# Layer B's step rebuilt: output product in four column quarters, new memory turned by VectorE, tails in batches of sixteen, softmax in stages

## The chip, the core and the metric

The kernel runs on one core of one Trainium2 chip. Five engines work side by side, each through its own instruction stream: TensorE (PE: matmuls, and PEld: the loads of the stationary operand), VectorE (DVE), ScalarE (ACT), GpSimd (POOL) and SyncE (SP), which issues the transfers here. SBUF is the working memory of 128 partitions, and TensorE writes to PSUM. The metric is the time on the device in microseconds (us); lower is better.

## What is computed

Two layers in turn, A B A B, each behind a LayerNorm and added to the residual `x` of 2048 tokens by 640. A is a linear-memory attention over four segments; the change hardly touches it. B is a recurrence over 64 segments of 32 tokens. Each segment sees 8 memory rows and its 32 tokens, 40 rows in all; 32 heads of 128:

```python
for s in range(n_seg):
    xs = x[:, s * seg_len:(s + 1) * seg_len, :].copy()
    h = jnp.concatenate([mem, xs], axis=1)
    q = jnp.einsum('btd,dhe->bhte', h, Wq)
    k = jnp.einsum('btd,dhe->bhte', h, Wk)
    v = jnp.einsum('btd,dhe->bhte', h, Wv)
    scores = jnp.einsum('bhqe,bhke->bhqk', q, k) * scale
    scores = jnp.where(mask[None, None], scores, -1000000000.0)
    p = _softmax(scores, axis=-1)
    o = jnp.einsum('bhqk,bhke->bhqe', p, v)
    o = jnp.einsum('bhte,hed->btd', o, Wo)
    mem = o[:, :M, :].copy()
    outs.append(o[:, M:, :])
```

The first 8 rows of a segment's output are the memory of the next one, so that the 64 steps of a layer can't be done side by side. What doesn't hang on the memory can: normalised tokens, and the projections of tokens whose place in the step is free.

## The kernel before

**Layer B, one step.** `layer_B` (L778) runs 64 steps. Step `s` finishes segment `s` while it projects 32 rows: the 8 memory rows of segment `s` beside the first 24 tokens of segment `s + 1`. The last 8 tokens of a segment, its *tail*, are projected ahead, in batches over several segments, and kept in DRAM. TensorE's order in a step is the order of the program text (`_OrdNC` chains each of TensorE, ScalarE, VectorE and GpSimd in that order):

1. `thin_mm`: keys and queries (`b_Ka`, `b_Qa`, `b_Kb`, `b_Qb`), each 20 matmuls of 512 columns, with 32 rows of the stationary operand in each of four column groups of the array; the column groups run side by side.
2. `transp4` and `scatter`: four blocks turned on TensorE (`b_TPak` and so on), copied by DVE (memory rows) and ACT (next segment's rows) into `QT` and `KT`.
3. `mask_mm` and `scores`: 128 small matmuls into two PSUM tiles `b_SP`, one for 16 heads each.
4. Softmax on DVE and ACT: for each tile maximum, subtraction and exponential, tile after tile; then sums, reciprocal, product (the second tile's on GpSimd, L1186 on), and `p_turn`, which turns the weights on DVE into `b_PTa` and `b_PTb`.
5. Meanwhile on TensorE values (`b_Va`, `b_Vb`) and one unit of tail projections (`tail_unit`, `b_tail`: 8 heads x 5 chunks, 64 columns = 8 segments x 8 tokens).
6. `pv`: weights by values (`b_OTP`, 64 matmuls), copied to `OTsb` by DVE and ACT.
7. `od_chunk(0)` (a part of the output product of four earlier segments' tails, `b_OPSd`), then the step's output product `o_mm` into `b_OPS` (L974): 64 matmuls of 320 columns. The 640 output columns are two halves of interleaved 64-column pieces. Four column groups of the array take two heads x two halves, so rows 0 to 63 and 64 to 127 of `b_OPS` hold partial sums that have still to be added. Then `od_chunk(1)`.
8. New memory: ACT copies `b_OPS` to `b_msb` in three parts, and small matmuls with a 0/1 matrix `selm` (`b_MT`) turn the memory rows and add the two partial sums (the *fold*), DVE writes them into the next step's columns (`b_HX`). In between stand pieces of `vtail_unit` (value projections of tails, 20 matmuls of 256 columns).
9. `x_out`: two adds on DVE (one for each half of the partial sums) with the residual rows `XO`, and two stores.

A tail unit's result is stored by `tail_evac` to `QKd` (DRAM, one row of 128 x 512 for each segment) and fetched a step ahead by `tails_load` into one buffer, from which GpSimd copies it into `QZ` and `KT` (`tails_copy`) behind its part of the softmax.

**LayerNorm for B** comes in groups of 128 tokens: `ln_load`, `ln_norm` (DVE, with one power on GpSimd between), and a step later `ln_spread` (five turns on TensorE, two copies on ACT into `HX`, the tokens, and `TX`, the tails).

**Entry of a layer B.** All 8 tail units of the first batch, then keys and queries of the first segment, `load_B_wo`, value tails, and the first steps; weights `wv` and `wo` are read again for each layer B, as their space serves layer A in between.

**Transfers** are issued on SP, one queue in order.

Of the kernel before, what the change touches and what calls it, by code (L numbers as in the profile page):

```python
# [37 lines left out]
def alloc_consts(tc, ctx):  # L38
# [10 lines left out]
    C.selm = cp.tile([128, 2, 8], BF16, name="b_sel")  # L49
# [122 lines left out]
def build_masks(G, C, pool):  # L172

    G.tensor_tensor(out=C.selm[:, 0, :], in0=C.identb[:, 24:32], in1=C.identb[:, 88:96], op=ALU.add)
    G.tensor_tensor(out=C.selm[:, 1, :], in0=C.identb[:, 56:64], in1=C.identb[:, 120:128], op=ALU.add)
# [70 lines left out]
def layer_A(nc, tc, C, W, x_src, x_dst, src_is_bf16, nseg=4, out_bf16=False, xb_dst=None, load_w=None, side_loads=None):  # L246
# [7 lines left out]
    with ExitStack() as ctx:  # L254
# [105 lines left out]
        def out_stage_b(n_, tt, halves=(0, 1)):  # L360
# [20 lines left out]
            xnb = w1l.tile([128, D], BF16, name="a_xnb")  # L381
            if n_ == nseg - 1:
                nc.scalar.copy(xnb[:], xnew[:])
            else:
                K("xnb").gpsimd.tensor_copy(xnb[:], xnew[:])
# [367 lines left out]

def load_B_resident(nc, W, B_Wq, B_Wk, k, after):

    c, r = divmod(k, 8)
    t, src = ((W.wk, B_Wk), (W.wq, B_Wq))[r % 2]
    h = r // 2
    nc.gpsimd.tensor_copy(t[0:1, c, 1024 * h:1024 * h + 1], after[0:1, 0:1])
    nc.sync.dma_start(t[:, c, 1024 * h:1024 * h + 1024], src[128 * c:128 * c + 128, 8 * h:8 * h + 8].rearrange("p h e -> p (h e)"))  # L760


def load_B_wv(nc, W, B_Wv):
    for c in range(NCH):
        nc.sync.dma_start(W.wv[:, c, :], B_Wv[128 * c:128 * c + 128].rearrange("p h e -> p (h e)"))
# [12 lines left out]
def layer_B(nc, tc, C, W, x_src, xb_src, x_dst, mem0, B_Wv, B_Wo, nsteps=64, out_bf16=False, tag=""):  # L778
# [4 lines left out]
    NT = nsteps // 8  # L783
    QKd = tc.dram_tile([nsteps, 128, 512], BF16, name=f"b_QKd{tag}")
    VTd = tc.dram_tile([nsteps, 8, 4096], BF16, name=f"b_VTd{tag}")
    with ExitStack() as ctx:
# [4 lines left out]
        hp = pool("b_hx", 4)  # L791
# [21 lines left out]
        mask5, selm = C.mask5, C.selm  # L813
        QZ = st.tile([128, 32, 32], BF16, name="b_QZ")
        HXz = st.tile([128, NCH, 1, 32], BF16, name="b_HXz")
        OTdef = [wk.tile([128, 32, 32], BF16, name=f"b_OTdef{i}") for i in range(2)]

        def init_state():
            XO_ = bx.tile([64, 320], F32, name="b_XO", tag="XO")
            nc.vector.memset(XO_[:], 0.0)  # L820
            XOd_ = bx.tile([64, 320], F32, name="b_XOd", tag="XOd")
# [20 lines left out]
        def ln_load(g, home=None):  # L842
            pool_, tg = home or (bx, "xt")
            xt = pool_.tile([128, D], BF16, name="b_xt", tag=tg)
            nc.sync.dma_start(xt[:], xb_src[128 * g:128 * g + 128, :])
            ln_xt[g] = xt

        def ln_norm(g):
            xt = ln_xt[g]
            f = layernorm_tile(nc, sml, C, xt[:], xt[:], "b_ln")  # L850
            if g in (0, 2) and not entered:
                info = mybir.DependencyInfo(mybir.DependencyClass.NoSync, mybir.DependencyReason.SCHED_ONLY)
                tc.add_manual_dep(f.ins, (C.after2 if g else C.after).ins.name, info, reason="order")
            ln_ready.append(g)

        def ln_spread(g):
            xt = ln_xt.pop(g)
# [3 lines left out]
            HX[g] = hp.tile([128, NCH, 4, 32], BF16, name="b_HX", tag="HX")  # L861
            T, half = divmod(g, 2)
            if half == 0:
                TX[T] = tx.tile([128, NCH, 8, 8], BF16, name="b_TX", tag="TX")
            nc.scalar.copy(TX[T][:, :, 4 * half:4 * half + 4, :], tps[:, :, :, 24:32])
            nc.scalar.copy(HX[g][:, :, :, 8:32], tps[:, :, :, 0:24])

        def cols_of(u):
            if u == nsteps:
                return HXz[:, :, 0, :]  # L870
            return HX[u // 4][:, :, u % 4, :]
# [26 lines left out]
        def tails_load(s):  # L898
            tl = bx.tile([128, 2, 32, 8], BF16, name="b_tl", tag="tl")
            nc.sync.dma_start(tl[:].rearrange("p a h t -> p (a h t)"), QKd[s])  # L900
            return tl

        def tails_copy(s, tl):
            nc.gpsimd.tensor_copy(QZ[:, :, 0:8], tl[:, 0, :, :])
            nc.gpsimd.tensor_copy(KT[s][:, :, 0:8], tl[:, 1, :, :])
# [9 lines left out]
        def tail_unit(T, k, i0, i1, shared=False):  # L915
            proj, hg = divmod(k, 4)
            Wt = W.wk if proj else W.wq
            if i0 == 0:
                if shared:
                    tail_ps[0] = ps_tile([128, 8, 64], F32, "b_tail")  # L920
                else:
                    tail_ps[0] = po.tile([128, 8, 64], F32, name="b_tail", tag="tail")
            ps = tail_ps[0]
            for i in range(i0, i1):
                h = 8 * hg + i
# [4 lines left out]
        def tail_evac(T, k, eng, home=None, dma=nc.sync.dma_start):  # L930
            proj, hg = divmod(k, 4)
            pool_, tg = home or (wk, "tu")
            tu = pool_.tile([128, 8, 8, 8], BF16, name="b_tu", tag=tg)
            evac(eng, tu[:].rearrange("p s h t -> p h s t"), tail_ps[0][:].rearrange("p h (s t) -> p h s t", t=8),
                 None if proj else SCB)
            o = 256 * proj + 64 * hg
            dma(QKd[8 * T:8 * T + 8, :, o:o + 64].rearrange("s p f -> p s f"), tu[:].rearrange("p s h t -> p s (h t)"))

        def vtail_unit(T, k, c0=0, c1=NCH, ps=None):
# [3 lines left out]
            for c in range(c0, c1):  # L943
                for q in range(4):
                    n = 2 * b4 + q // 2
                    nc.tensor.matmul(ps[32 * q:32 * q + 32, :], lhsT=TX[T][:, c, 4 * (q % 2):4 * (q % 2) + 4, :].rearrange("p s t -> p (s t)"),
# [21 lines left out]
        def wo_half(h, jj2):  # L968
            return W.wo[:, h, :].rearrange("p (c j x) -> p j c x", j=2, x=64)[:, jj2]

        def d_half(rows, jj2):
            return rows.rearrange("t (c j x) -> t j c x", j=2, x=64)[:, jj2]
# [12 lines left out]
        n0 = min(4, NG)  # L985
        for g in range(n0):
            ln_load(g, homes[g])
        load_B_wv(nc, W, B_Wv)
        for g in range(2):
            ln_norm(g)  # L990
        for g in range(2):
            ln_spread(ln_ready.pop(0))
        nc.gpsimd.memset(HX[0][:, :, 0, 0:8], 0.0)
        with nc.allow_non_contiguous_dma(reason="mem0 transpose load (tiny)"):
            for c in range(NCH):
                nc.sync.dma_start(HX[0][:, c, 1, 0:8], mem0[:, 128 * c:128 * c + 128].rearrange("t p -> p t"))
        for k in range(8):
            tail_unit(0, k, 0, 8, shared=True)
            tail_evac(0, k, "act" if k % 2 == 0 else "dve", (((kqp, "kq"),) * 4 + ((w2, "QT"), (w2, "KT"), (wk, "tu"), (w2, "Vth")))[k])
            if k in (0, 2) and n0 > 2:  # L1000
                ln_norm(2 + k // 2)
            if k in (5, 7) and ln_ready:
# [17 lines left out]
        tails_copy(0, tails_load(0))  # L1020
# [7 lines left out]
        if NT > 1:  # L1028
            tail_unit(1, 0, 0, 8, shared=True)
# [3 lines left out]
        def x_out(ops_, XO_, store, nm):  # L1033
            nc.vector.tensor_tensor(out=XO_[:], in0=ops_[0:64, :], in1=XO_[:], op=ALU.add)
            if out_bf16:
                xo = wk.tile([64, 320], BF16, name=f"b_xnb{nm}", tag=f"xnb{nm}")
            else:
                xo = XO_
# [335 lines left out]
```

## Time and profile before

| what | value |
|---|---|
| runs of the kernel | 2619.58, 2614.66, 2613.08 us; median 2614.66 |
| the profiled execution | 2617.2 us |
| its span, first to last instruction | 2615.5 us |
| mean granted TensorE clock | 0.998 |
| first `b_Ka` of the two layers B | 377.7 and 1682.3 us |
| last `b_Ka` of the two layers B | 1287.4 and 2593.6 us |
| the clean step from 510.58 to 524.73 us | 14.15 us: PE busy 14.00, DVE 7.67, ACT 7.24, POOL 1.69 |

Durations come from the profiled execution. A matmul's duration reaches from its start to its modelled end, and matmuls overlap; what a row of matmuls costs PE is read from the distance of their starts. In a timeline a line joins neighbouring instructions of one form: start, time to the end of the last, engine, line of the helper that issued it (L109 for nearly all of layer B), operation, tile written and tiles read, count, and in brackets the idle time ahead of it and what ended it. "issue" there means that the profile shows nothing for which the engine waited. In a row of the groups, the numbers behind the bar are the total busy time in us and the mean duration of one in ns, and behind the second bar the idle time before them.

### The profile page before, as it was taken

The page shows a single profiled execution, that of the slowest core. Times are in us where ns is not written, and L with a number is a line of the kernel's source. Part 1 is how long each engine was busy: PE and PEld are TensorE (multiplying, and loading weights), DVE is VectorE, ACT ScalarE, POOL GpSimd, SP SyncE. Part 2 cuts the span into 40 slices and gives each one's busy share as a digit, 9 for nine tenths or more (in the row PEclk, how much of TensorE's full clock was granted, in tenths as well). Part 3 has the DMA queues.
Part 4 walks back from the last instruction along what each step waited for, and adds up shares of the span by engine and source line. Part 5 has one row for each costly group of instructions (what it writes and reads, how often), then busy time and mean ns, then how long its engine had stood idle before and what let it go on. Part 6 is the DMA issues. An engine that isn't in the chain of part 4 may idle for free.

```text
span 2615.5 us, 144745 instructions
## 1 busy us (share of the span) xinstructions
PE 2492.2 (95%) x64608; PEld 1652.4 (63%) x64608; DVE 1706.5 (65%) x4690; ACT 1529.1 (58%) x3462; POOL 699.0 (27%) x1507
## 2 busy tenths in 40 slices
PE   7999989999999999999989999899999999999998
PEld 5566566666666666666655665666666666666665
DVE  8999855555555555555679998455655555555555
ACT  6988944545555554544379888455545454545443
POOL 5777621111111111111146776111111111111110
PEclk9999999999999999999999999999999999999999
DMA  4122362222222222221220113622222122222110
GB/s 159 46 79 77 103 210 47 46 43 44 48 46 46 47 44 47 41 44 30 64 81 22 63 52 104 200 42 43 43 43 46 41 44 42 43 41 42 39 27 20
DMA packets 325201, 156.21 MB, mean 60 GB/s; under 512 B 245856, under 2 KB 309472, under 8 KB 322784
## 3 DMA queue, kind: packets, MB, share of 16 engines
q1 hardware_dynamic: 324576, 146.95, 22.4%
q8 instruction: 505, 8.27, 1.4%
q14 instruction: 120, 0.98, 0.1%
HBM read 95.15 MB, written 51.71 MB: 56 GB/s over the span
## 4 chain that ended last, share of the span: by engine, by line
PE 64%; DVE 23%; ACT 7%; issue 3%; DMA 2%; SPq 0%; DVEq 0%; POOL 0%; ACTq 0%; POOLq 0%
PE b_OPS L109 11%; DVE a_nm L138 6%; PE b_Ka L109 5%; PE b_Qb L109 5%; PE b_Kb L109 5%; PE b_Qa L109 5%; PE b_vtail L109 3%; PE b_OPSd L109 3%; PE b_SP L109 3%; DVE b_SP L109 3%; ACT a_PT L138 3%; PE a_S L109 2%; DVE b_negmax L109 2%; PE b_OTP L109 2%; DVE b_PTa L109 2%
## 5 line engine op out<-in xcount | busy, mean ns | idle before, releaser
L109 PEld LDWEIGHTS <-b_HX 128*32 128x32 bf16 x15360 | 440.0, 96 | 323.8 <-issue 4.2
L109 POOL TENSOR_TENSOR b_Pn<-b_E,b_rs 128x200 bf16<-128x200 bf16 x128 | 78.0, 609 | 1388.4 <-DVE b_rs L109 1120.5
L138 DVE TENSOR_REDUCE a_nm<-a_S 128x2 f32<-128x512 f32 (+3 forms) x512 | 395.0, 816 | 32.8 <-PE a_S L109 25.2
L138 ACT ACTIVATE a_PT<-a_T 128x1024 bf16<-128x1024 f32 (+1 forms) x384 | 344.9, 902 | 31.6 <-PE a_T L109 23.7
L109 PE MATMUL b_OPS<-b_wo,b_OTsb 128*32 128x320 bf16 x8192 | 305.0, 299 | 3.6 <-issue 2.8
L109 PEld LDWEIGHTS <-b_OTsb 128*32 128x32 bf16 x8192 | 207.1, 96 | 79.3 <-issue 6.5
L109 DVE CAST b_HX<-b_MT 128x8 bf16<-128x8 f32 x372 | 63.8, 172 | 262.9 <-PE b_MT L109 257.6
L138 POOL TENSOR_SCALAR_AFFINE_SELECT a_PT<-a_PT 128x256 bf16<-128x256 bf16 x380 | 187.9, 503 | 128.2 <-ACT a_PT L138 127.2
L109 ACT CAST b_msb<-b_OPS 128x64 bf16<-128x64 f32 x378 | 69.4, 256 | 225.6 <-PE b_OPS L109 225.6
L109 ACT CAST b_kq<-b_Kb 128x512 bf16<-128x512 f32 x128 | 74.9, 585 | 201.7 <-PE b_Kb L109 201.7
L109 DVE COPY b_KT<-b_TPak 128x128 bf16<-128x128 bf16 x128 | 28.7, 225 | 228.3 <-PE b_TPak L109 228.3
L109 DVE TENSOR_SCALAR b_kq<-b_Qa 128x512 bf16<-128x512 f32 x128 | 88.6, 692 | 123.2 <-PE b_Qa L109 120.3
L109 PE MATMUL b_Ka<-b_wk,b_HX 128*32 128x512 bf16 x2520 | 160.4, 379 | 1.8 <-issue 1.4
L109 PE MATMUL b_Va<-b_wv,b_HX 128*32 128x512 bf16 x2520 | 161.6, 380 | 0.0
L109 PE MATMUL b_Vb<-b_wv,b_HX 128*32 128x512 bf16 x2520 | 161.2, 379 | 0.0
L109 PEld LDWEIGHTS <-b_kq 128*128 128x128 bf16 x2080 | 116.9, 98 | 69.3 <-ACT b_kq L109 55.0
L109 PE MATMUL b_Qa<-b_wq,b_HX 128*32 128x512 bf16 x2520 | 159.8, 379 | 0.0
L109 PE MATMUL b_Kb<-b_wk,b_HX 128*32 128x512 bf16 x2520 | 159.7, 379 | 0.0
L109 PE MATMUL b_Qb<-b_wq,b_HX 128*32 128x512 bf16 x2520 | 159.7, 379 | 0.0
L109 DVE CAST b_OTsb<-b_OTP 128x160 bf16<-128x160 f32 (+1 forms) x384 | 133.9, 377 | 29.2 <-PE b_OTP L109 8.5
L109 ACT ACTIVATE b_E<-b_SP 128x200 bf16<-128x200 f32 x256 | 86.3, 337 | 106.9 <-DVE b_SP L109 105.1
L109 PE MATMUL b_vtail<-b_wv,b_TX 128*32 128x256 bf16 x2880 | 135.8, 271 | 5.2 <-issue 5.0
(206 smaller groups left out, 5478.5 us busy)
## 6 DMA issues: line engine op xcount, KB each, us to landing
b_QKd<-b_tu SPq DMA_DIRECT2D x128, 128.0 KB
b_tl<-b_QKd SPq DMA_DIRECT2D x128, 128.0 KB
b_wv<-in_B_Wv_dram SPq DMA_DIRECT2D x10, 1024.0 KB
b_wo<-in_B_Wo_dram SPq DMA_DIRECT2D x16, 640.0 KB
b_Vth<-b_VTd SPq DMA_DIRECT2D x512, 16.0 KB
b_XO<-xres SPq DMA_DIRECT2D x256, 30.0 KB
b_VTd<-b_vt SPq DMA_DIRECT2D x224, 32.0 KB
xres<-a_xnew SPq DMA_DIRECT2D x19, 320.0 KB
```

Of the source, the lines that this page charges most:

```text
L109: r = f(*a, **k)
L138: r = f(*a, **k)
```

## The change

**Output product.** Each head's product goes to the four column groups of the array as four quarters of 160 columns; all heads add up in place. `b_OPS` and `b_OPSd` are [128, 160], row 32 q + t holding token t's quarter q, with no partial sums: 128 matmuls of 160 columns in a step in place of 64 of 320, and 16 in place of 8 in each `od_chunk` part.

**New memory.** DVE copies the first 64 columns of `b_OPS` to `b_msb`, ACT the other 96, and DVE turns `b_msb` in 32 by 32 blocks straight into the next step's columns; the turn also writes 24 columns of tokens that have been used already. The rows of the model dimension are held in another order for that (chunk c, partition 32 q + x is row 160 q + 32 c + x), so the weights of K, Q and V are loaded in that order and layer A writes its bf16 copy of `x` in that order. `selm` and the fold are gone. `b_vtail` stands in one piece behind the output products.

**Tails.** Batches are of 16 segments: a unit is 4 heads, 20 matmuls of 128 columns. 16 units stand ahead of the first step. `QKd` is laid out by unit, so that a store writes 1 KB pieces and a load, now for two segments and issued every second step, reads 128-byte pieces. LayerNorm groups of tokens (every four steps) and of tails (every 16) are apart.

**Softmax.** Both maxima, then both subtractions, then both exponentials.

**Residual rows.** `XO` is loaded whole by one transfer; results go out by four stores in place of two, after one add.

```diff
+            turned = xnb[:].rearrange("p (c q x) -> p q c x", q=4, x=32)
+            plain = xnew[:].rearrange("p (q c x) -> p q c x", q=4, x=32)
...
-                K("xnb").gpsimd.tensor_copy(xnb[:], xnew[:])
+                K("xnb").gpsimd.tensor_copy(turned, plain)
...
+def b_rows(src, c):
+
+    return src.rearrange("(q c x) h e -> c q x h e", q=4, x=32)[c]
...
-    NT = nsteps // 8
+    NT = nsteps // 16
+    NV = nsteps // 8
...
+        def cols_of(u, back=0):
+            t_, i = (HXz, 0) if u == nsteps else (HX[u // 4], u % 4)
+            return t_[:, :, 24 + 32 * i - back:56 + 32 * i - back]
...
         def tails_load(s):
-            tl = bx.tile([128, 2, 32, 8], BF16, name="b_tl", tag="tl")
-            nc.sync.dma_start(tl[:].rearrange("p a h t -> p (a h t)"), QKd[s])
+            tl = bx.tile([128, 2, 8, 2, 4, 8], BF16, name="b_tl", tag="tl")
+            T, i = divmod(s, 16)
+            nc.sync.dma_start(tl[:].rearrange("p a q s h t -> p (a q) (s h t)"), QKd[T][:, :, i:i + 2, :].rearrange("p k s f -> p k (s f)"))
             return tl
...
-            for i in range(i0, i1):
-                h = 8 * hg + i
+            for i in range(4):
+                h = 4 * hq + i
...
-        def o_mm(ops_, src_ap_fn, hpairs, first, last):
-            for n_, h0 in enumerate(hpairs):
-                for e in range(2):
-                    for jj2 in range(2):
-                        k = 2 * e + jj2
-                        nc.tensor.matmul(ops_[32 * k:32 * k + 32, :].rearrange("p (c x) -> p c x", x=64), lhsT=src_ap_fn(h0 + e), rhs=wo_half(h0 + e, jj2),
-                                         start=(first and n_ == 0), stop=(last and n_ == len(hpairs) - 1),
-                                         tile_position=(0, 32 * k), skip_group_check=True)
+        def o_mm(ops_, src_ap_fn, hs, first, last):
+            for n_, h in enumerate(hs):
+                for q in range(4):
+                    nc.tensor.matmul(ops_[32 * q:32 * q + 32, :], lhsT=src_ap_fn(h), rhs=W.wo[:, h, 160 * q:160 * q + 160],
+                                     start=(first and n_ == 0), stop=(last and n_ == len(hs) - 1),
+                                     tile_position=(0, 32 * q), skip_group_check=True)
...
-        for k in range(8):
-            tail_unit(0, k, 0, 8, shared=True)
...
+        for k in range(16):
+            tail_unit(0, k, shared=True)
...
-            nc.vector.tensor_tensor(out=XO_[:], in0=ops_[0:64, :], in1=XO_[:], op=ALU.add)
...
+            nc.vector.tensor_tensor(out=xo[:], in0=ops_[:], in1=XO_[:], op=ALU.add)
...
-            for b, SP in ((0, SPa), (1, SPb)):
-                soft_max(b, SP)
-                soft_sub(b, SP)
-                soft_exp(b, SP)
+            for f in (soft_max, soft_sub, soft_exp):
+                for b, SP in ((0, SPa), (1, SPb)):
+                    f(b, SP)
...
-            if ln_xt_due(s):
-                ln_norm(ln_g(s))
...
-                for ca, cb in parts:
-                    nc.scalar.copy(msb[:, 64 * ca:64 * cb], ops[:, 64 * ca:64 * cb])
-                for pi, (ca, cb) in enumerate(parts):
-                    mt = ps_tile([128, cb - ca, 8], F32, f"b_MT{pi}")
...
-                    nc.vector.tensor_copy(dst[:, ca:cb, 0:8], mt[:])
-                    vtail_some((1, 1, NCH)[pi])
...
+            if ln_due(s):
+                ln_norm(ln_due(s))
+
             if not last:
+                msb = wk.tile([128, 160], BF16, name="b_msb", tag="msb")
+                dst = cols_of(u + 1, 24)
+                nc.vector.tensor_copy(msb[:, 0:64], ops[:, 0:64])
+                nc.scalar.copy(msb[:, 64:160], ops[:, 64:160])
+                for ca, cb in ((0, 2), (2, NCH)):
+                    nc.vector.transpose(out=dst[:, ca:cb, :], in_=msb[:, 32 * ca:32 * cb].rearrange("p (c k) -> p c k", k=32))
+            vps = vtail_unit(vwork[0], vwork[1]) if vwork else None
+            if vunit:
+                vtail_evac(vunit[0], vunit[1], vps, "act")
```

More of the change, by code (lines that the diff above doesn't have):

```diff
@@ L983, in layer_B @@
         entered = []
         homes = [(bx, "xt"), (bx, "XO"), (bx, "XOd"), (bx, "tl")]
-        n0 = min(4, NG)
-        for g in range(n0):
-            ln_load(g, homes[g])
+        for key, home in zip((("T", 0), ("H", 0), ("T", 1), ("H", 1)), homes):
+            ln_load(key, home)
         load_B_wv(nc, W, B_Wv)
-        for g in range(2):
-            ln_norm(g)
-        for g in range(2):
+        ln_norm(("T", 0), C.after)
+        ln_norm(("H", 0))
+        for _ in range(2):
             ln_spread(ln_ready.pop(0))
-        nc.gpsimd.memset(HX[0][:, :, 0, 0:8], 0.0)
+        nc.gpsimd.memset(cols_of(0)[:, :, 0:8], 0.0)
@@ L994, in layer_B @@
         with nc.allow_non_contiguous_dma(reason="mem0 transpose load (tiny)"):
             for c in range(NCH):
-                nc.sync.dma_start(HX[0][:, c, 1, 0:8], mem0[:, 128 * c:128 * c + 128].rearrange("t p -> p t"))
-        for k in range(8):
-            tail_unit(0, k, 0, 8, shared=True)
[L999 to L1002, printed above, removed]
+                for q in range(4):
+                    o = 160 * q + 32 * c
+                    nc.sync.dma_start(cols_of(1)[32 * q:32 * q + 32, c, 0:8], mem0[:, o:o + 32].rearrange("t x -> x t"))
@@ L1063, in od_chunk @@
                 OTd = OTdef[(od["s0"] // 4) % 2]
-                pairs = [8 * k + 2 * p_ for p_ in range(4)]
+                hs = list(range(8 * k, 8 * k + 8))
                 if part is not None:
-                    pairs = pairs[2 * part:2 * part + 2]
-                o_mm(od["ps"], lambda h: OTd[:, h, :], pairs, k == 0 and part != 1, k == 3 and part != 0)
+                    hs = hs[4 * part:4 * part + 4]
+                o_mm(od["ps"], lambda h: OTd[:, h, :], hs, k == 0 and part != 1, k == 3 and part != 0)
                 if part != 0:
@@ L1075, in od_begin, with ln_due @@
         def od_begin(s0, xo, tag="opsd"):
[L1076 to L1082 removed]
+            od.update(s0=s0, n=0, xo=xo, ps=po.tile([128, 160], F32, name="b_OPSd", tag=tag))
+        def ln_due(s):
+            key = ("H", s // 4 + 2) if s % 4 == 1 else ("T", s // 16 + 2) if s % 16 == 11 else None
+            return key if key and key[1] < (NG if key[0] == "H" else NT) else None
         for s in range(nsteps):
```

169 lines of the change are left out of this document (70 added, 99 removed).

## The prediction

> **What bounds the kernel now.** I read the page first, then one layer-B step in the timeline, then the times between the starts of `b_Ka` (one a step), then the stops in PE's stream.
>
> ```profile
> span 2615.5 us, 144745 instructions
> ...
> PE 2492.2 (95%) x64608; PEld 1652.4 (63%) x64608; DVE 1706.5 (65%) x4690; ACT 1529.1 (58%) x3462; POOL 699.0 (27%) x1507
> ...
> q8 instruction: 505, 8.27, 1.4%
> ...
> PE 64%; DVE 23%; ACT 7%; issue 3%; DMA 2%; SPq 0%; DVEq 0%; POOL 0%; ACTq 0%; POOLq 0%
> PE b_OPS L109 11%; DVE a_nm L138 6%; PE b_Ka L109 5%; PE b_Qb L109 5%; PE b_Kb L109 5%; PE b_Qa L109 5%; PE b_vtail L109 3%; PE b_OPSd L109 3%; PE b_SP L109 3%; DVE b_SP L109 3%; ACT a_PT L138 3%; PE a_S L109 2%; DVE b_negmax L109 2%; PE b_OTP L109 2%; DVE b_PTa L109 2%
> ```
>
> TensorE sets the end, and layer B holds most of it: from the first to the last `b_Ka` 909.7 us in the one layer B and 911.3 in the other, 126 step distances of 14.45 us on average. The commonest distance is 14.15, so 0.3 a step is something else. The 505 instruction packets are 16 KB each (8.27 MB); TensorE has 129,216 loads and matmuls, 256 for each packet. A clean step, from `b_Ka` at 510.58 to the next at 524.73:
>
> ```profile
> 518.42 0.34 ACT L109 ACTIVATE b_E<-b_SP 128x200 bf16<-128x200 f32 x1 [0.38 <-DVE b_SP L109]
> 518.78 0.36 DVE L109 TENSOR_REDUCE b_ssum<-b_E 128x5 f32<-128x200 bf16 x1 [0.20 <-ACT b_E L109]
> ...
> 520.91 0.27 PEld L109 LDWEIGHTS <-b_Vth 32*128 32x128 bf16 x32 [0.18 <-DVE b_PTb L109]
> ...
> 521.50 2.35 PE L109 MATMUL b_OPS<-b_wo,b_OTsb 128*32 128x320 bf16 x64
> ...
> 523.96 0.55 ACT L109 CAST b_msb<-b_OPS 128x64 bf16<-128x64 f32 x3 [1.74 <-PE b_OPS L109]
> ...
> 524.46 0.56 DVE L109 CAST b_HX<-b_MT 128x8 bf16<-128x8 f32 x3 [2.37 <-PE b_MT L109]
> ...
> 524.73 1.25 PE L109 MATMUL b_Ka<-b_wk,b_HX 128*32 128x512 bf16 x20
> ```
>
> PE waits in two places: before the second half of `b_OTP` for `b_PTb`, the end of the softmax chain on DVE, which itself waited at 518.78 for the second exponential; and after the output product, for copy, fold and cast. In other steps PE stops in mid stream with nothing to wait for:
>
> ```profile
> 550.09 2.20 PE L109 MATMUL b_OPS<-b_wo,b_OTsb 128*32 128x320 bf16 x57
> ...
> 553.38 0.12 PEld L109 LDWEIGHTS <-b_OTsb 128*32 128x32 bf16 x7 [1.42 <-issue]
> 553.38 0.45 PE L109 MATMUL b_OPS<-b_wo,b_OTsb 128*32 128x320 bf16 x7 [1.09 <-issue]
> ```
>
> Between this stop (551.99) and the like one at 596.06 the trace has 2558 loads and matmuls, 10 x 256 less 2. Between those at 2084.60 and 2129.12 it has 2558 again. At 551.99 the packet for the next 256 instructions ran from 550.49 to 551.96, and PE went on at 553.37, 1.41 us after it; at the other three the distance is 1.57, 1.44 and 1.42. So PE has its instructions in blocks of 256, the next block's packet starts only when it enters a block, and no block may be run in less than the time of that refill. There are 35 such stops of over 0.3 us in the 126 steps, 23.1 us together, 0.18 a step. The refill, counted from entering a block in `b_OTP` or `b_OPS`: 1.15 us to the packet's start (median), 1.1 for it (median 1.116), 1.4 after it: **3.65 us** (single ones 3.1 to 4.3). In slow stretches (`b_Kb`, `b_Vb`) the packet starts up to 0.8 before PE itself gets there, so about 2.5 there.
>
> **The change, part by part** (a step, against 14.15).
>
> Softmax in stages. DVE does both maxima, both subtractions, then the sums. Two dependent pairs lose their gap (end to start 0.10; independent ones overlap by 0.09): second subtraction from 517.95 to about 517.59, second exponential 518.06 to 518.40 (after the first, which starts near 517.77), second sum 518.42 in place of 518.78. All behind it moves along: **-0.36**, bounds 0 and -0.36. It holds if PE gets there in time: tail start 8.54 into the step, 20 matmuls of 128 columns at 56 ns (the row of `b_TPaq`: 4 in 0.22) are 1.12 in place of 40 x 29.4 ns = 1.18, 0.12 to the first `b_OTP` as today, 0.23 for its half: 10.01. `b_PTb` was ready at 10.42 and comes at 10.06, so the shorter tail itself is worth nothing.
>
> Output product. 64 matmuls of 320 columns become 128 of 160, four column groups at a time: groups of four now start 136 ns apart (320 columns are 133.3 of it), so 32 groups x (66.7 + 2.7) = 2.22 against 2.17: **+0.05**; each `b_OPSd` part stays at 0.28. Weight loads don't hold this up: four pairs of `b_SP` (40 columns) start every 25 ns, 6.25 a pair, and 17.3 are needed. The Trainium skill (TensorE: MATMUL & The Clock Gate, Part 1) says that starts never come closer than about 25 ns. By that rule 128 matmuls need 3.2; the row refutes it for column groups, whose starts lie 2 to 4 ns apart.
>
> Step's end. Today 1.05 from the last output matmul to `b_Ka`: `b_OPSd` 0.27, `b_vtail` and the fold's 20 matmuls 0.78. New: the copy can start 0.28 after PE has issued the product (as `b_msb` does), DVE copies 64 columns, turns 64, and `b_Ka` reads.
>
> ```profile
> L109 DVE STREAM_TRANSPOSE b_PTb<-b_Pn 128x64 bf16<-128x64 bf16 x128 | 26.0, 203 | 0.0
> ...
> L109 DVE CAST b_HX<-b_MT 128x8 bf16<-128x8 f32 x124 | 20.7, 167 | 249.8 <-PE b_MT L109 249.7
> ...
> L109 DVE CAST b_OTsb<-b_OTP 128x160 bf16<-128x160 f32 x256 | 83.0, 325 | 29.2 <-PE b_OTP L109 8.5
> ...
> L109 ACT CAST b_msb<-b_OPS 128x64 bf16<-128x64 f32 x126 | 26.7, 212 | 225.6 <-PE b_OPS L109 225.6
> ```
>
> Between 8 and 160 columns DVE pays 1.04 ns a column, so 64 cost 0.23: 0.28 + 0.23 + 0.10 + 0.20 + 0.06 = 0.87, and PE is covered for 0.28 + 20 x 27.3 ns = 0.83. ACT's 96 columns (0.25) and the second turn end by about 1.02, needed at 1.3. So 0.88 in place of 1.05: **-0.17**, bounds -0.22 (PE alone) and +0.1 (each of the three DVE steps 0.1 dearer). The two adds of `x_out` (0.48 each) become one of 160 columns (0.33); DVE is idle there, nothing gained.
>
> Sum so far -0.48, x 126 = -60 us.
>
> **Instruction supply.** A step has 852 loads and matmuls today (160 K and Q, 36, 128 scores, 80 V, 80 tail, 128 `b_OTP`, 32 `b_OPSd`, 128 `b_OPS`, 80 `b_vtail` and fold). The change: -40 tail, -40 fold, +128 and +32: 932, and the added ones run at 8.7 ns each. I ask how long the next 256 take from each place, against the refill. Method, on today's code: from the start of `b_OTP` 0.76 + 0.28 + 112 x 17 ns = 2.94 against 3.5 (0.55 short), from its end 3.9 (none); mean 0.27 over these 128 and 0.25 over 40 of the tail, divided by 256: 0.17 a step, where 0.18 is measured. New code: from the start of `b_OTP` (0.58 now) 0.58 + 0.28 + 96 x 8.7 ns = 1.69, 1.8 short; from `b_OPSd` 0.28 + 224 x 8.7 ns = 2.23, 1.4 short; from the start of `b_OPS` 2.22, 1.4; from its middle 1.11 + 0.28 + 0.55 + 56 of `b_Ka` 1.5 = 3.45, 0.2. Means: 1.6 over 128, 1.4 over 32, 0.9 over 128, 0.7 over the last 20 of the tail: (205 + 45 + 115 + 14) / 256 = 1.5 a step, as block edges fall everywhere alike (932 is no multiple of 256). **+1.3** over today, all on PE's path, x 126 = +164. With 3.1 for the refill it is 0.9 a step, with 4.3 2.4.
>
> LayerNorm steps. Its chain on DVE (464.13 to 466.59) now stands ahead of the copy, which wants to start at 466.07: 0.5 late in some 32 steps of both layers, half of it covered where PE stopped in the product: **+8**, bounds 0 and 16, with the 5 turns (0.29) of 8 more groups among them.
>
> Entry. 16 tail units stand ahead of the first step in place of 8: 8 x 1.12 = 9.0 a layer. Part covers waits of today: the first scores waited 0.95 for `b_tl`, the first `b_OTP` 1.3 for `b_Vth`, and in the second layer the first step is 3.0 over the rest. **+13**, bounds 6 and 20.
>
> At nothing: the tails' packets change places (store 1024 of 128 B, load 128 of 1 KB; now the other way, every second step; 1024 took 1.0 us in the trace, and the load has a step's time); SP's queue: four stores of `xres` for two, one load of `b_XO` for two, 1.7 us more in a queue that idles 3 of 14; permuted weight rows (as many packets as long); POOL's permuted `a_xnb` (0.72 of an engine 27% busy). If POOL's tail copies came late, scores would wait.
>
> **Sum**: 2617.2 - 60 + 164 + 8 + 13 = 2742 for an execution like the profiled one (span 2615.5 and 1.7 around it). The median shown is 2.5 lower, 2614.66, so **2740**.
>
> **Rivals.** *The refill keeps up* (faster). Most of the 505 block edges pass today unnoticed, and the four stops may be late packets only. Then -60, LayerNorm 16, entry 13: 2584. It decides if a block of 256 can be run in 2.2 us. Against it: of hundreds of edges none was passed sooner than 1.1 us after its packet's end. The Trainium skill (Runtime: NRT & Kernel Launch, Instruction fetch mechanics) describes two lines of 256 instructions, the next fetched while one runs, and calls the cost of an edge mostly hidden. By this rule the time is this rival's; the trace agrees with the two lines, and its 23.1 us disagree with the hiding. 0.12.
> *The narrower matmuls don't overlap in their column groups*, and each takes the 25 ns of a whole group of `b_SP`: product 128 x 25 ns = 3.2, `b_OPSd` 0.8 for 0.56, +1.2 a step, stops down to about 0.8: 2800. That `b_SP` and `b_OPS` do overlap speaks against it: 0.03.
> *The gains fail*: DVE is late with the new memory by 0.5 in every step and the stages bring nothing: (0.36 + 0.17 + 0.1) x 126 = 79 more, 2820. For it: DVE is now in that chain three times. 0.07.
> *They cancel*: stops of 0.5 a step in all, refill 2.5 everywhere as in slow stretches: 2615. 0.03.
> My forecast 0.75.
>
> The likeliest's own range is 2690 to 2795; toward the cancelling and the failing cases I give **2650 to 2810**. Faster by over 0.3% (8 us, what can be told from no change here) 0.12, within 0.03, slower 0.85.
>
> **What would show it.** PE's stops named "issue" some 1.4 us long in `b_OPS` and the parts beside it, nearly every step, 256 instructions apart, about 545 instruction packets; `b_Ka` to `b_Ka` near 15.3 on average with the shortest near 13.7; `b_PTb` 0.36 earlier; `b_OPS` groups 69 ns apart where unbroken; entry 6 later a layer. It is wrong if `b_OPS` runs through in 2.2 us with no stops.

## The result, and the profile after

The changed kernel takes 2807.64 us (median of 4 runs, 2805.6 to 2814.09), the kernel before 2617.12 in the runs taken beside it (2613.08 to 2624.91). The ratio is 1.0728, 95% interval 1.0696 to 1.0761: slower by 7.3%. The prediction was 2740 with a range of 2650 to 2810: the direction is right, the time lies at the upper end of the range, 68 us over the forecast.

The page of the changed kernel, lines that answer to those shown of before: span, engines (busy us, share, instructions), the instruction packets (count, MB, share) and the engines' shares of the chain that ended last.

```profile
span 2804.6 us, 154910 instructions
...
PE 2505.3 (89%) x69744; PEld 1795.8 (64%) x69808; DVE 1624.0 (58%) x4576; ACT 1484.4 (53%) x3178; POOL 704.4 (25%) x1513
...
q8 instruction: 545, 8.93, 1.3%
...
PE 73%; DVE 10%; issue 6%; DMA 5%; ACT 5%; POOL 0%; SPq 0%; DVEq 0%; ACTq 0%; POOLq 0%
...
L108 PE MATMUL b_OPS<-b_wo,b_OTsb 128*32 128x160 bf16 x16384 | 325.1, 233 | 83.8 <-issue 82.4
```

The last of these lines, as it was in the kernel before:

```profile
L109 PE MATMUL b_OPS<-b_wo,b_OTsb 128*32 128x320 bf16 x8192 | 305.0, 299 | 3.6 <-issue 2.8
```

TensorE is busy about as long as before (2505 us for 2492) in a span that is 189 us longer, so the time went into its idle stretches. Beside TensorE's own share two shares of the chain grew: "issue", from 3% to 6%, and DMA, from 2% to 5%. They are two different losses. The clock is not a third one in the steps: in the steps of both kernels it was granted in full, and the stretches at half speed (0.981 on average over the whole span, 0.998 before) all lie outside them: in layer A, in the entry and at a layer's end. 545 instruction packets are what the prediction counted, and `b_OPS` waited 82.4 us for "issue" where it waited 2.8 before.

The first loss, in TensorE's timeline of one step (start and duration in us; in brackets the idle time before, and what ended it):

```profile
592.55 0.47 PE L108 MATMUL b_OTP<-b_PTb,b_Vth 32*128 32x40 bf16 x32
592.95 0.46 PE L108 MATMUL b_OPSd<-b_wo,b_OTdef 128*32 128x160 bf16 x16
593.24 1.07 PE L108 MATMUL b_OPS<-b_wo,b_OTsb 128*32 128x160 bf16 x52
596.04 1.50 PE L108 MATMUL b_OPS<-b_wo,b_OTsb 128*32 128x160 bf16 x76 [1.74 <-issue]
597.37 0.45 PE L108 MATMUL b_OPSd<-b_wo,b_OTdef 128*32 128x160 bf16 x16
597.65 0.72 PE L108 MATMUL b_vtail<-b_wv,b_TX 128*32 128x256 bf16 x20
598.19 1.04 PE L108 MATMUL b_Ka<-b_wk,b_HX 128*32 128x512 bf16 x16
```

After 52 of 128 matmuls TensorE stands still for 1.74 us. The instruction packet of that moment ran from 593.79 to 594.74, and TensorE went on at 596.04, 1.30 after its end, as at the stops of the kernel before. I count a stop where two starts on TensorE are over 0.3 us apart and it goes on 1.0 to 1.8 us after the end of a packet. So counted, the 126 step distances hold 168 stops with 180.8 us, and 78 with 38.3 us in the kernel before. The count takes in some waits for data that happen to end in that time: 38 stops of the kernel before (13.6 us) and 20 of the changed one (7.9 us) end with data, mostly with ScalarE's copy to `b_kq`. Without them about 173 us stand against 25.

The second loss is where layer A (its stretch is called stage A in what follows) ends and layer B begins, once in each layer B. The chain of waits between 328 and 386 us (start, duration, what):

```profile
330.66 30.86 DMA xres_bf<-a_xnb
...
361.64 0.73 POOL a_xnb L137
...
362.76 21.62 DMA b_xt<-xres_bf
384.39 0.02 issue
384.41 0.90 DVE b_ln_st L108 x2
```

The store of one tile of 160 KB takes 31 us to land, and the reload for layer B's LayerNorm 22. In the kernel before, none of the 55 longest pieces of this chain between 312 and 350 us is a transfer. In the same stretch SyncE's queue shows what it issued just behind the store:

```profile
330.66 0.32 SPq L385 DMA_DIRECT2D xres_bf<-a_xnb  x1
331.02 13.81 SPq L769 DMA_DIRECT2D b_wv<-in_B_Wv_dram  x1
352.96 0.32 SPq L377 DMA_DIRECT2D xres<-a_xnew  x1
```

It is a load of `b_wv`, whose rows the change permutes. How busy the 16 transfer engines were while these loads ran (tenths of their time and GB/s, in 40 slices): first the kernel before from 316 to 338 us, then the changed one from 324 to 384.

```profile
DMA  0003859999998989989989999749996898999976
GB/s 0 0 0 45 194 253 447 417 402 447 417 462 372 381 354 395 513 352 440 411 335 429 439 417 444 320 169 374 230 379 166 351 343 313 362 345 327 328 244 195
```

```profile
DMA  2248242222222222222382322252546343222221
GB/s 49 71 140 240 94 160 98 93 98 109 109 98 109 109 99 106 106 98 109 152 291 103 119 104 100 109 191 112 172 146 195 104 134 136 104 104 109 104 88 51
```

Before, nearly all engines move packets, mostly at 300 to 450 GB/s; afterwards the row reads 2 (that is 20 to 30%) at about 100 GB/s. Adding up the packets of the trace gives the same: 16.2 in flight before and 4.0 after, while the packets are 8 KB long both times and take as long (0.31 us, median).

The packets of the store itself show what it waits for. It has 128 of 1280 bytes: 96 of them ran at 331 us, and 32 from 357 to 360, as the third load, issued ahead of the store, came to its end (the 384th packet of 8 KB ran at 358). So three quarters of the store moved at once, and one quarter stood behind the loads.

Where the 189.1 us between the two spans are, by the starts of `b_Ka` and of the first `b_lntps` (the first turn of layer B's LayerNorm) in each layer:

| part | foretold | measured |
|---|---|---|
| 126 steps without their stops (stages, product, step's end, LayerNorm) | -60 + 8 | -60.1 |
| stops for instructions in these steps | +164 | +142.5 |
| entry, first `b_lntps` to first `b_Ka` (32.7 and 34.8 before, 44.3 and 41.0 after) | +13 | +17.8 |
| end of stage A: the first `b_lntps` is later by 42.5 and 41.6 | 0 | +84.1 |
| after the last `b_Ka` | 0 | +4.7 |

The steps together are 1903.3 us for 1820.9 (15.11 on average for 14.45).

### The profile page after: what moved, and what is told of

Same layout as the page of the kernel before. It is cut to its first block, busy times and chain, and to the rows that moved or that the text cites. A ratio compares the mean times of both kernels' runs of the same rounds, so it can differ in the third digit from the quotient of the medians.

```text
span 2804.6 us, 154910 instructions
## 1 busy us (share of the span) xinstructions
PE 2505.3 (89%) x69744; PEld 1795.8 (64%) x69808; DVE 1624.0 (58%) x4576; ACT 1484.4 (53%) x3178; POOL 704.4 (25%) x1513
## 4 chain that ended last, share of the span: by engine, by line
PE 73%; DVE 10%; issue 6%; DMA 5%; ACT 5%; POOL 0%; SPq 0%; DVEq 0%; ACTq 0%; POOLq 0%
PE b_OPS L108 11%; PE b_tail L108 6%; PE b_Ka L108 5%; PE b_Qa L108 5%; DVE a_nm L137 5%; PE b_Kb L108 5%; PE b_Qb L108 5%; PE b_Va L108 5%; PE b_Vb L108 5%; PE b_SP L108 4%; PE b_OPSd L108 3%; PE b_vtail L108 3%; PE b_OTP L108 3%; ACT a_PT L137 2%; PE a_S L108 2%
## 5 line engine op out<-in xcount | busy, mean ns | idle before, releaser
L108 PEld LDWEIGHTS <-b_HX 128*32 128x32 bf16 x15360 | 492.1, 96 | 305.3 <-issue 30.2
L108 PE MATMUL b_OPS<-b_wo,b_OTsb 128*32 128x160 bf16 x16384 | 325.1, 233 | 83.8 <-issue 82.4
L108 PEld LDWEIGHTS <-b_OTsb 128*32 128x32 bf16 x16384 | 291.3, 97 | 100.6 <-issue 97.6
L108 ACT CAST b_msb<-b_OPS 128x96 bf16<-128x96 f32 x126 | 30.2, 239 | 361.7 <-DVE b_msb L108 359.4
L137 POOL TENSOR_SCALAR_AFFINE_SELECT a_PT<-a_PT 128x256 bf16<-128x256 bf16 x380 | 189.1, 506 | 127.7 <-ACT a_PT L137 124.4
L108 PE MATMUL b_Ka<-b_wk,b_HX 128*32 128x512 bf16 x2520 | 169.0, 380 | 13.1 <-issue 11.9
L108 DVE CAST b_msb<-b_OPS 128x64 bf16<-128x64 f32 x126 | 28.1, 223 | 262.5 <-PE b_OPS L108 262.5
L108 PE MATMUL b_Qa<-b_wq,b_HX 128*32 128x512 bf16 x2520 | 167.5, 379 | 4.2 <-issue 2.6
L108 PE MATMUL b_Qb<-b_wq,b_HX 128*32 128x512 bf16 x2520 | 166.1, 379 | 0.0
L108 ACT CAST b_kq<-b_Ka 128x512 bf16<-128x512 f32 x128 | 75.0, 586 | 131.1 <-PE b_Ka L108 131.1
L108 PE MATMUL b_OPSd<-b_wo,b_OTdef 128*32 128x160 bf16 x4096 | 122.8, 237 | 23.8 <-issue 23.8
```

The costliest lines, as they stand in the source:

```text
L108: r = f(*a, **k)
L137: r = f(*a, **k)
```

## The experiments

Ratios are to the kernel before, run on the same chip beside the kernel named.

### The loads of b_wv in four pieces each

```diff
-        nc.sync.dma_start(W.wv[:, c, :], b_rows(B_Wv, c).rearrange("q x h e -> q x (h e)"))
+        for q in range(4):
+            nc.sync.dma_start(W.wv[32 * q:32 * q + 32, c, :], b_rows(B_Wv, c)[q].rearrange("x h e -> x (h e)"))
```

> The changed kernel, with each of the five loads of b_wv issued as four loads of 32 partitions in place of one load whose source steps through four blocks of rows. Theory: the one load with four outer rows moves only four packets at a time (13 packets of 8 KB per us from 331 us on, against 30 to 47 in the kernel before), the stores and reloads of the last segment of stage A queue behind it, and this is the 42 us by which the first b_lntps is late in each layer. Then the first b_Ka comes at about 390 us in place of 431.8, the transfers run some 16 at a time again, and the time is 2807.6 - 2 x 42 = about 2724 (2705 to 2745). Rival 1: what holds the entry is the permuted copy of a_xnb or the tails' units, not the loads: 2808, first b_Ka at 430. Rival 2: twenty issues in SP's queue in place of five, at 0.5 to 1 us each, hold the reloads behind them: a part of the gain, 2750 to 2790.

2742.19 us, ratio 1.05 (1.0476 to 1.0524), and a span 61.8 us shorter than that of the changed kernel. The first `b_lntps` comes at 353.6 in place of 387.5 (345.0 before the change), and in the second layer 2 us late in place of 42: 73 us gained. But the first `b_Ka` came at 404.4 and not at 390: the entry itself grew from 44.3 to 50.8 us, and from 41.0 to 51.2 in the second layer. The waits of this kernel between 350 and 404 us (us in total, times, longest) show what for:

```profile
ACT b_tu L108 <- DMA b_QKd<-b_tu: 10.5, 1, 10.5
DVE b_tu L108 <- DMA b_QKd<-b_tu: 9.6, 1, 9.6
PE b_tail L108 <- ACT b_tu L108: 9.0, 2, 5.9
```

The sixteen units of tails share eight buffers, so the ninth waits until the store of the first has landed, and on SyncE's queue nine of the twenty `b_wv` loads were issued at 366 us, just ahead of the first of these stores. The theory is right on the lateness of stage A's end, and the time lies within its range; the second rival is right on a part: 16.7 us are given back in the entry. In the first layer 8.6 us of lateness are left (353.6 for 345.0).

### The permuted loads alone, in the kernel before

```diff
-        nc.sync.dma_start(W.wv[:, c, :], B_Wv[128 * c:128 * c + 128].rearrange("p h e -> p (h e)"))
+        nc.sync.dma_start(W.wv[:, c, :], B_Wv.rearrange("(q c x) h e -> c q x h e", q=4, x=32)[c].rearrange("q x h e -> q x (h e)"))
```

> The kernel before, with nothing changed but the source rows of the five loads of b_wv: the four blocks of 32 rows that the changed kernel loads together (so V is computed with its weight rows in another order than its input). Theory that the loads alone make the 42 us a layer: 2617 + 84 = 2701 (2680 to 2720), four packets at a time from about 318 us on, first b_Ka near 420. Rival, that something else of the change is needed for it (the permuted a_xnb, the other order of reloads): 2617 within 0.5%.

2691.11 us, ratio 1.0302 (1.0285 to 1.0319): +78.5 us, with nothing else of the change. The first `b_lntps` is 39.8 and 41.1 us later in the two layers, and the steps are as before (14.40 on average). These loads alone make 80.9 of the 84.1 us of lateness.

### Two and eight blocks of rows

As above, with `q=8, x=16` and `q=2, x=64`.

> The kernel before, with the rows of each load of b_wv taken as eight blocks of 16 rows (V's weight rows in another order than its input). Theory that a load keeps as many packets in flight as its source has outer blocks: 8 at a time, some 24 packets of 8 KB per us, the 640 packets take 27 us in place of the 50 and more with four blocks, and the first b_lntps comes 0 to 15 us later than before: 2615 to 2645, so well under the 78 us of four blocks. Rival, that any permuted source is as slow as another (by its third dimension): 2690, four at a time.

> As the run with eight blocks, with two blocks of 64 rows. Theory: 2 packets at a time, some 6 per us, the 640 packets take about 105 us, the first b_lntps some 95 to 100 us late in each layer: 2815 (2760 to 2860). Rival, any permuted source is as slow as another: 2690.

| outer blocks of the source | packets in flight (median) | first `b_lntps` later by | time against before |
|---|---|---|---|
| none (128 rows in order) | 16.2 | 0 | 1 |
| 8 | 8.1 | 14.8 and 20.9 us | 1.0144 (1.0129 to 1.0159), +37.6 us |
| 4 | 4.06 | 39.8 and 41.1 | 1.0302 (1.0285 to 1.0319), +78.5 |
| 2 | 2.03 | 83.2 and 85.2 | 1.0636 (1.0617 to 1.0655), +167 |

The second column is the median over the time of the loads, all packets counted. As many packets are in flight as the source has outer blocks, and each halving of the blocks somewhat more than doubles the lateness (35.7, 80.9 and 168.4 us for both layers). The rival, that any permuted source costs the same, falls. The store `xres<-a_xnew` issued behind the first two loads tells the same of the transfers behind them: of its 128 packets 64 came late with eight blocks (12 us behind the others), 32 with four (in the changed kernel), and 16 with two (22 us behind). That is 8, 4 and 2 sixteenths of it, as if the loads held that many of the sixteen transfer engines; the trace doesn't name a packet's engine. Both sizes were somewhat off (2655 for at most 2645; 2784 for 2815, inside its bounds). The chain of waits with two blocks names the same two transfers as above, now longer:

```profile
339.91 43.20 DMA xres_bf<-a_xnb
389.26 11.40 SPq L386
400.71 24.35 DMA b_xt<-xres_bf
```

The Trainium skill (DMA: Bandwidth & Descriptors, "Why a DMA increments its semaphore by 16 and not by 1") has this as a rule: a transfer uses the largest number of engines up to 16 that divides the slowest dimension of both access patterns. For 2, 4, 8 and 128 that is 2, 4, 8 and 16; the trace agrees with 2.03, 4.06, 8.1 and 16.2.

### Four pieces in the kernel before, and the stores on another queue

The kernel before, with each `b_wv` load issued as four of 32 partitions (same rows, same places):

> The kernel before, with each load of b_wv issued as four loads of 32 partitions of its own rows (the same data in the same places). It tells what is left of the entry's loss when the blocks are loaded one by one. Theory, that twenty issues spread over SP's queue come late enough to stand before the entry's stores of b_tu: +4 to +10 a layer, 2625 to 2640. Rival, that what was left came from the sixteen units alone: 2617 within 0.3%.

2640.39 us, ratio 1.0088 (1.0073 to 1.0103). Stage A's end is on time in the first layer (345.3) and 2 us late in the second, and the entry is 8.4 and 8.0 us longer: the theory, just over its upper end. The waits of the first entry fit it: VectorE's for a store of `b_tu` are 9.0 us in place of 4.0, ScalarE's 7.8 in place of 3.0. The steps took 5 us more in all, no more than one run differs from the next. So what the first experiment left over in the entry has two parts, twenty issues in place of five and the sixteen units.

The changed kernel with four loads a chunk, and the entry's stores of `b_tu` on ScalarE's queue:

```diff
-            tail_evac(0, k, "act" if k % 2 == 0 else "dve", tu_homes[k % 8])
+            tail_evac(0, k, "act" if k % 2 == 0 else "dve", tu_homes[k % 8], nc.scalar.dma_start)
```

> The changed kernel with four loads a chunk for b_wv (2742) and with the entry's tail stores (b_QKd<-b_tu) issued on ScalarE's queue in place of SP's. In the run with four loads ScalarE and VectorE waited 10.5 and 9.6 us in the first entry for a store of b_tu to land, with nine loads of b_wv issued just ahead of the stores on the same queue, and the entry took 50.8 us from the first b_lntps to the first b_Ka in place of 44.3. Theory: on another queue the stores do not stand behind the loads, the entry falls to about 41 us: 2742 - 2 x 10 = 2722 (2708 to 2735). Rival: the stores share the sixteen DMA engines with the loads whatever the queue and land as late: 2742 (2735 to 2750).

2747.8 us, ratio 1.0491 (1.0477 to 1.0508): no gain over 1.05. The mechanism was there, smaller than hoped: VectorE's wait for the stores fell from 9.6 to 5.0 us, ScalarE's 10.5 is gone, and the entry fell to 46.8 and 46.9 us, 8 less in all. But the steps took 15.16 us on average in place of 15.07, 12 more in all, 9.7 of them in stops for instructions by the count above (185.3 us for 175.6). Why the stops grew is not shown; the four runs with four loads a chunk differ by 15 us among themselves, so the 12 may not belong to the edit.

### More instructions for the same product

The kernel before, each matmul of the output product made as two of half the columns:

```diff
-                        nc.tensor.matmul(ops_[32 * k:32 * k + 32, :].rearrange("p (c x) -> p c x", x=64), lhsT=src_ap_fn(h0 + e), rhs=wo_half(h0 + e, jj2),
...
+                        for y in range(2):
+                            nc.tensor.matmul(ops_[32 * k:32 * k + 32, :].rearrange("p (c x) -> p c x", x=64)[:, :, 32 * y:32 * y + 32], lhsT=src_ap_fn(h0 + e), rhs=wo_half(h0 + e, jj2)[:, :, 32 * y:32 * y + 32],
...
```

> The kernel before, with every matmul of the output product (b_OPS and b_OPSd) made as two of half the columns: 128 of 160 columns a step in place of 64 of 320, the same sums, 160 instructions of TensorE a step more (852 to 1012). Theory of the instruction supply (256 instructions in a packet, 3.65 us from one refill to the next): b_OPS runs through 256 instructions in about 2.2 us and stops once a step for 1.2 to 1.5 us as in the changed kernel, 2617 + 126 x 1.3 = 2781 (2750 to 2815), and PE's stops named issue stand in b_OPS. Rival 1: the same columns stream in the same time and the supply keeps up: 2617 within 0.5%. Rival 2: each narrow matmul costs more in the array itself: as slow, but with evenly longer distances between the groups of b_OPS and no stops.

2831.55 us, ratio 1.0839 (1.0823 to 1.0855): +219 us. The page of this kernel:

```profile
q8 instruction: 584, 9.57, 1.4%
...
PE 62%; DVE 21%; issue 9%; ACT 7%; DMA 1%; POOL 0%; DVEq 0%; ACTq 0%; SPq 0%; POOLq 0%
...
L109 PE MATMUL b_OPS<-b_wo,b_OTsb 128*32 128x160 bf16 x16384 | 336.9, 234 | 115.2 <-issue 114.6
L109 PEld LDWEIGHTS <-b_OTsb 128*32 128x32 bf16 x16384 | 297.4, 97 | 137.5 <-issue 134.9
```

The arithmetic and the bytes of data are those of before; 79 packets of instructions are more, and `b_OPS` waits for "issue" as the theory says. The steps are 212.5 us longer, and 197 of them are stops (202 stops, 235.4 us, for 78 and 38.3). The expectation of 1.3 us a step was 0.3 too low, and the time lies above its range; a likely reason is that in the changed kernel 80 other instructions a step go, here none. The second rival, dearer matmuls without stops, is left the other 15 us. A step has 1012 here, 932 in the changed kernel, 852 before.

### Fewer instructions in the changed kernel

```diff
                 for q in range(4):
+                    if q > 1 and not (first and n_ == 0) and not (last and n_ == len(hs) - 1):
+                        continue
                     nc.tensor.matmul(ops_[32 * q:32 * q + 32, :], lhsT=src_ap_fn(h), rhs=W.wo[:, h, 160 * q:160 * q + 160],
```

> The changed kernel with two of the four column quarters of the output product left out for all heads but the first and the last of each sum (so half of the output's columns lack 30 of 32 heads): 75 matmuls and 75 weight loads a step fewer, 932 to 782 instructions; the groups of the other two quarters keep their 69 ns if the quarters run side by side. Theory of the instruction supply: the stops of PE behind an instruction packet (168 stops, 180.8 us in the steps of the changed kernel, 78 and 38.3 before) fall back to about those of the kernel before, 2807.6 - 142 = 2666 (2640 to 2690), and a step takes about 13.97 us. Rival 1: what slows the steps is not the supply but the turn on VectorE, LayerNorm ahead of it, or the other order: 2790 to 2810. Rival 2: the quarters do not run side by side, so half of the product's 2.2 us goes as well: 2530 to 2570.

2654.86 us, ratio 1.0135 (1.012 to 1.015). A step takes 13.94 us on average where 13.97 was expected, with 65 stops of 24.7 us, of which 15.4 end with data. Its page:

```profile
q8 instruction: 470, 7.70, 1.2%
...
L108 PE MATMUL b_OPS<-b_wo,b_OTsb 128*32 128x160 bf16 x8704 | 317.8, 233 | 4.2 <-issue 3.0
```

The product itself still takes 2.2 us of a step (in the twenty-first, from 10.73 to 13.1 us after the first `b_Ka`), so half its matmuls gone made it no shorter; the quarters run side by side, and what was saved are the stops. `b_OPS` waits 3.0 us for "issue" in place of 82.4. Its steps are 65 us shorter in all than those of the kernel before; that it is still slower sits in the entry and stage A's end, where this kernel has the permuted loads (first `b_lntps` at 386.4).

### The softmax stages, alone and undone

In the kernel before:

```diff
-            for b, SP in ((0, SPa), (1, SPb)):
-                soft_max(b, SP)
-                soft_sub(b, SP)
-                soft_exp(b, SP)
+            for f in (soft_max, soft_sub, soft_exp):
+                for b, SP in ((0, SPa), (1, SPb)):
+                    f(b, SP)
```

> The kernel before, with the softmax of the two halves in stages (both maxima, both subtractions, both exponentials) as in the changed kernel, and nothing else. Theory, by the prediction's term of 0.36 us a step: b_PTb is 0.36 us earlier, 2617 - 126 x 0.36 = 2572 (2560 to 2585). Rival 1: the time comes back at a later wait in the step (ScalarE's order, or an instruction refill that the shorter step meets): 2600 to 2617. Rival 2: the first half's exponential comes later by more than the second gains, and PE waits there: 2617 to 2640.

2583.85 us, ratio 0.9886 (0.9871 to 0.99): faster than before by 28.7 us, where 45 were foretold. `b_PTb` ends 9.97 us into a step (median) for 10.29: 0.32 earlier, nearly the 0.36 of the prediction. The clean step is 13.87 for 14.15, 0.28 shorter, and the weight loads of `b_OTP` now run through without a wait for `b_PTb`. So the term was 0.08 too large. By the count above the stops fell too, to 25.7 us from 38.3.

The same edit undone in the changed kernel:

> The changed kernel with the softmax halves one after the other again, as before the change. In the kernel before, stages alone were worth 28.7 us. Theory that in the changed kernel the refills set much of the pace, so that an earlier b_PTb is partly given back in a longer stop in b_OPS: 2808 to 2825, with fewer microseconds of stops than 180.8. Rival: the gain is independent of the supply: 2807.6 + 29 to 45 = 2837 to 2853, with the same stops.

2848.12 us, ratio 1.0871 (1.0854 to 1.0887) where the changed kernel has 1.0728: some 37 us slower, the rival's number. The stops are 189.4 us for 180.8, so the instruction supply doesn't take the gain back, and my theory here is wrong. It fits that the stops come in the fast stretch behind the softmax, whenever it starts.

### Everything but the product in quarters

The kernel before with tails of sixteen segments and the softmax in stages, its own output product, fold, memory turn and row order:

> The kernel before with the tails of sixteen segments a batch and the softmax in stages, but with its own output product, fold, memory turn and row order of weights and input: the change without the product in quarters. Against the staged kernel (2584) the tail unit is 0.13 us shorter a step (20 matmuls of 128 columns in place of 40 of 64, -17 us) with 40 instructions fewer, and the entry has 16 units in place of 8 (+6 to +9 a layer). Theory: 2584 - 17 + 16 = 2583 (2565 to 2600). Rival 1: fewer instructions a step also take away stops (25 us in the staged kernel): 2555 to 2570. Rival 2: the entry's second eight units wait for the stores of the first eight, +15 or more a layer: 2600 to 2615.

2585.5 us, ratio 0.9866 (0.985 to 0.9883), the theory's number. Its steps take 14.05 us (14.15 with stages alone) with 17.6 us of stops, and its entry is 13.1 and 5.3 us longer than before (45.8 and 40.1), about what the longer tails cost it in the changed kernel. Against the staged kernel its steps are 13 us shorter in all, 8 of them stops, and its entries 16 longer. So the tails of sixteen give in the steps nearly what they take in the entry. This kernel and the staged one both beat the kernel before and the changed one; their intervals overlap, and they can't be told apart.

## Why the prediction was right in direction and 68 us short

**The step's gains** (-60, and +8 for LayerNorm, -52 together) came out at -60.1 without the stops, and a step takes 13.94 us once its instructions are fewer. The shortest steps are 13.55 to 13.65 (13.7 foretold). That the gains' own sum fits so well is partly luck, as two misses cancel. The stages give 0.28 in the clean step of the kernel before, where 0.36 was foretold. The step's end gives 0.25 where 0.17 was: from the end of the last group of output matmuls to `b_Ka` (counted as in the prediction, one group distance behind the group's start) it is 0.80 us (median) in place of 1.05. No run shows LayerNorm's 8 by itself.

**The narrower matmuls overlap** in their column groups, as foretold, so the rival of 2800 us by a slower array is out: unbroken groups of four start 69 ns apart, the number foretold, and half of the matmuls left out made the product no shorter.

**Instruction supply** (+164) is the mechanism that slows the steps, shown from both sides: 160 instructions more in the kernel before cost 219 us, 150 fewer in the changed kernel saved about 153. The term was 22 too large by the count above (142.5 us, 1.13 a step for 1.3), and 16 too large without the waits for data (148). It is well inside the bounds that the refill's spread gave it. The Trainium skill's rule that the edge between two instruction blocks is mostly hidden (Runtime: NRT & Kernel Launch, Instruction fetch mechanics) held for the slow stretches of a step and not for the product: of the 180.8 us of stops 98 stand in `b_OPS`.

**The entry** (+13) came out at +17.8, within its bounds of 6 and 20; the tails of sixteen make +18.4 in the kernel that has everything but the product in quarters.

**What failed** is a clause of the line "at nothing": "permuted weight rows (as many packets as long)". The packets are as many and as long, and still the loads are slower, because what was not asked is how many of them move at a time: 4 in place of 16. 84 us went there, 80.9 with these loads alone: the five loads of `b_wv` in each layer run in the last 60 us of stage A, and its last stores and layer B's first reloads come behind them, a quarter of each store's packets after the loads' own. What is left of the span's growth without this 84 is 105 us, where the prediction had 125. The loads of `b_wk` and `b_wq` are permuted in the same way, earlier in the first stage A; no run changed them alone. There the changed kernel is 6 us late already before the first load of `b_wv` is issued (323.1 us for 317.1, and as late with four loads a chunk), and what makes these 6 stays open.

That the time still lies in the stated range is luck. The range of the foretold mechanism ended at 2795; it had been widened to 2810 for the case in which the step's gains fail, and they did not fail.

## What to carry to other kernels

Before calling a reordered load free, look at the outermost dimension of its access pattern: the number of blocks there (2, 4 or 8) was the number of packets in flight here, and the price was paid by the stores and reloads behind the load. Count the instructions of a fast stretch against the refill: the prediction read some 3.65 us for 256 instructions from the stops before the change, and the added stops that it worked out from this were right within a seventh. So cutting matmuls in half for a better layout can cost more than the layout saves. Where a change has several parts, try them apart: of those tried here the smallest one (three lines of softmax order) was the only clear gain. The product in quarters and the turned memory were not tried apart.

## What the runs showed of the hardware that was not expected

A transfer of 128 rows of 8 KB whose source has 2, 4 or 8 outer blocks kept 2.03, 4.06 and 8.1 packets in flight, and 16.2 with its rows in order. The same 1 MB as four transfers of 32 partitions ran with about 16 packets in flight again (125 packets of 8 KB in 4 us at 368 us in the kernel with four loads a chunk).

"Issue" in a list of waits isn't always instruction supply. In stage A of the changed kernel the weight loads of TensorE show one such wait of 16.27 us, ended at 350.91, the longest of that kernel. The trace has no instruction packet between 329.2 and 357.5, and in the same stretch the matmuls of `a_YP` waited up to 16.2 us for `a_xnew` on VectorE, which had waited 17.1 us for a transfer. A restart 1.0 to 1.8 us after the end of an instruction packet is the sign of a stop for instructions, but not a proof: in the kernel before about half of the stops with this distance end with data for which TensorE waited anyway. Both are needed, the packet and the absence of such data.
